# One-hot positions laid out contiguously, the last converted weights made early, and the fetch of the lower keys written a round later, in a kernel of attention, routed experts and a shared FFN

## The chip, the cores and the metric

The kernel runs on one core of one Trainium2 chip. A core has five engines that each work through an instruction list of their own in order: TensorE (matrix products and the loads of their stationary weights), VectorE, ScalarE, GpSimd and SyncE, which here only issues transfers. Sixteen DMA engines move data between the chip's memory and the core's SBUF. The metric is the device time of one execution in microseconds, lower is better.

## What is computed

```python
def reference(**kwargs):
    attn_out = _attn_ref(**attn_kwargs)            # B, H, S, D = 4, 8, 576, 64
    B, H, S, D = attn_out.shape
    x = np.ascontiguousarray(attn_out.transpose(0, 2, 1, 3)).reshape(B * S, H * D)
    x = _moe_ref(x=x, **moe_kwargs)
    return _moe2_ref(x=x, **moe2_kwargs)

def _moe_ref(x, w_gate, w1, w2):
    N, D = x.shape                                  # 2304, 512
    E = w_gate.shape[1]                             # 8
    cap = N // E                                    # 288
    flat = (x @ w_gate).flatten()
    order = np.argsort(-flat)
    ...                                             # greedy: best pair first, each token once, cap tokens an expert
    for e in range(E):
        mask = assigned == e
        h = np.maximum(x[mask] @ w1[e], 0.0)        # 512 x 1024
        out[mask] = h @ w2[e]

def _moe2_ref(x, w_in, w_out):
    h = x @ w_in                                    # 512 x 2048
    relu6 = np.clip(h + 3.0, 0.0, 6.0)
    g = h * relu6 / 6.0
    return g @ w_out
```

The attention is causal and has a second, linear part (`M_prev`, `z_prev`) mixed in by a gate. The weights of the experts and of the shared FFN arrive as 64-bit words, and those of the FFN are turned into 32-bit ones by the kernel.

## The kernel before

The attention takes the first 295 us or so; then the first round of the routing, and from about 335 us on eight rounds, one for each expert that is settled in turn. Round `s` has two kinds of steps: eight of kind 0 (one block of 128 of the expert's 1024 hidden columns each) on its 288 tokens, then `y_in`, which copies the expert's output out of PSUM into four tiles `y`, then sixteen of kind 1 (a block of the shared FFN each). Every step multiplies into `h`, makes `g` from `h` on ScalarE, VectorE and GpSimd (`t` and `pc` on ScalarE, lines 1210 and 1211, `g` on VectorE, line 1212), and multiplies `g` into four accumulators `acc`. Round 0 works with whole fp32 weights `raw`, straight from their transfers, and on the side splits those of the FFN into a high and a low part (`split_w`: `w` or `WB`, ScalarE line 1105, GpSimd line 1106), which the later rounds fetch again (`w<-hl`, line 1102) or keep (`WB`). Later rounds use such pairs throughout.

Of the FFN's 32 weight tiles, 28 are converted during the attention and lie in DRAM as `wb`. The last four (steps 14 and 15) are converted in round 0 itself: `cv.rest` loads one (line 975), four VectorE instructions make its bits (lines 981 to 984), ScalarE its sign (line 990, `wa`), GpSimd the product (line 991). The list `conv` holds these four, and each step of the loop takes one from it (line 1317). `load` puts them in the list when the step's place among the four `raw` places is its turn; their outputs are these `raw` tiles.

The routing of round `s + 1` is a generator, `Router.phase`, that is advanced a bit in each step of round `s`. Its parts here: the keys of each expert are made (from round 2 on in `by_dram`: matmul `rw`, ScalarE copy `ks` line 759, a transfer `kd` line 760, and two transfers that broadcast the upper and the lower halves to all partitions, `rHw` and `rLw`, line 763, all issued by SyncE); `search` then finds each expert's bound in four passes over `rHw` and four over `rLw`, each a `rcmp` of 128 x 2304 on VectorE (line 715) with a few small ones behind it; then positions, and `ids_units`. That has `u0`, which makes `ua` and the one-hot tile `oc` (row name `roc`, line 936, in two halves), and `u2`, which multiplies them in 20 matmuls of a 128 x 96 weight and a 6-column operand (recorded at the helper's line 702). Its result, by lines 945 to 949, is `ids`, the token numbers; the tokens are then gathered (`xg`) and transposed (`x_in`). Also there: the next `rX` (line 695), its transposes `rx`, and their copy `rXT` (line 747).

The order of each engine's instructions is made by a scheduler that works from the order of the code, its own estimates of time and the places that tiles wait for. Engines wait for each other through semaphores.

## Time and profile before

| | us |
|---|---|
| runs | 1116.09, 1106.57, 1122.56 |
| median | 1116.09 |
| profiled execution, its own time | 1115.67 |
| its span in the profile | 1113.9 |
| TensorE busy | 972.9 |
| VectorE busy | 637.6 |
| GpSimd busy | 625.4 |
| ScalarE busy | 587.8 |

A row of the timeline has the start, the duration, the engine, the line, the operation, output<-inputs and how many instructions of that kind follow each other; a bracket at its end is the time that the engine stood idle before it and what it waited for. "Granted clock" is TensorE's, as a share of 2.4 GHz; 0.5 is its lower level, 1.2 GHz.

### The profile page before, as it was taken

The numbers are of one execution on the slowest core, as the hardware profiler recorded it, in microseconds if no ns is written. First come the engines' busy times: TensorE is split into PE (matmuls) and PEld (weight loads), VectorE is DVE, ScalarE is ACT, GpSimd is POOL, SyncE is SP. The second block draws the span as 40 slices with busy tenths as digits, with TensorE's granted clock in tenths as the row PEclk, the third lists the DMA queues.
The fourth block names the chain that finished last, engine by engine and source line by source line (L and its number), as shares of the span: only waits on it lengthen the run. The fifth ranks groups of instructions, "written<-read, shape, count | busy, mean of one in ns | idle before, by whom it ended". The sixth has DMA issues, their size and how long they took to land.

```text
span 1113.9 us, 19553 instructions
## 1 busy us (share of the span) xinstructions
PE 972.9 (87%) x6556; PEld 876.5 (79%) x6556; DVE 637.6 (57%) x1587; ACT 587.8 (53%) x1471; POOL 625.4 (56%) x595
## 2 busy tenths in 40 slices
PE   3899888988419798789989999799999999999997
PEld 3677666766317586589989989799899999999996
DVE  8688996897682956971873684566385300200300
ACT  5777786876312343344554563465445356456453
POOL 7657656671410464663675685476557458558454
PEclk9899999999658899788999999999999999999998
DMA  6888877887223577447628726823942741751540
GB/s 156 228 251 226 254 226 221 255 234 198 72 77 102 166 244 207 153 128 231 175 73 257 202 76 220 199 76 127 259 138 74 235 170 58 256 184 58 190 153 22
DMA packets 125011, 190.23 MB, mean 171 GB/s; under 512 B 22128, under 2 KB 72688, under 8 KB 124912
## 3 DMA queue, kind: packets, MB, share of 16 engines
q1 hardware_dynamic: 121152, 179.54, 54.1%
q0 software_dynamic: 3072, 9.44, 2.9%
q8 instruction: 52, 0.85, 0.3%
q14 instruction: 47, 0.39, 0.1%
q10 hardware_dynamic: 688, 0.02, 0.0%
HBM read 144.60 MB, written 25.61 MB: 153 GB/s over the span
## 4 chain that ended last, share of the span: by engine, by line
PE 56%; DVE 15%; DMA 10%; POOL 7%; issue 5%; ACT 4%; SPq 2%; POOLq 0%; DVEq 0%; ACTq 0%
PE h L1221 7%; PE h L1222 6%; PE h L1224 6%; PE acc L1115 6%; PE acc L1116 6%; PE acc L1114 6%; PE h L1198 3%; DMA w<-hl 3%; PE acc L1251 3%; PE rp L702 3%; DVE rcmp L715 2%; PE av L328 2%; POOL gl L1244 2%; POOL t L1242 2%; PE sc L246 1%
## 5 line engine op out<-in xcount | busy, mean ns | idle before, releaser
L1106 POOL TENSOR_TENSOR w<-raw,w 128x512 fp32r<-128x512 f32 x128 | 168.1, 1325 | 108.4 <-ACT w L1105 107.8
L1242 POOL TENSOR_TENSOR t<-t,pc 128x288 f32<-128x288 f32 x112 | 92.0, 823 | 110.6 <-ACT t L1241 110.6
L1115 PE MATMUL acc<-gl,w 128*128 128x288 f32 x448 | 131.8, 304 | 9.0 <-POOL gl L1244 9.0
L1235 DVE TENSOR_TENSOR gl<-t,gh 128x288 fp32r<-128x288 f32 x56 | 37.6, 675 | 172.4 <-ACT gh L1234 169.3
L1116 PE MATMUL acc<-gh,w 128*128 128x288 f32 x448 | 130.0, 300 | 0.0
L1114 PE MATMUL acc<-gh,w 128*128 128x288 f32 x448 | 114.8, 310 | 1.7 <-DVE yo L1156 1.7
L1105 ACT ACTIVATE w<-raw 128x512 fp32r<-128x512 f32 x128 | 80.0, 632 | 57.9 <-PE acc L1116 26.7
L1239 ACT ACTIVATE t<-h,rthree 128x288 f32<-128x288 f32 x112 | 56.1, 501 | 99.2 <-PE h L1224 72.2
L1244 POOL TENSOR_TENSOR gl<-t,gh 128x288 fp32r<-128x288 f32 x112 | 91.1, 819 | 30.7 <-ACT gh L1243 30.7
L282 ACT ACTIVATE P<-P,mx 128x128 f32<-128x128 f32 (+2 forms) x144 | 83.7, 582 | 39.2 <-DVE mx L267 37.0
L1115 PEld LDWEIGHTS acc<-gl,w 128*128 128x128 f32 x448 | 86.6, 193 | 12.1 <-POOL gl L1244 11.8
L1116 PEld LDWEIGHTS acc<-gh,w 128*128 128x128 f32 x448 | 86.5, 193 | 0.0
L1114 PEld LDWEIGHTS acc<-gh,w 128*128 128x128 f32 x448 | 79.0, 196 | 3.4 <-DVE yo L1156 2.4
L1243 ACT ACTIVATE gh<-t 128x288 fp32r<-128x288 f32 x112 | 49.7, 444 | 58.3 <-POOL t L1242 58.0
L246 PE MATMUL sc<-kh,qs 128*128 128x128 f32 (+3 forms) x128 | 50.0, 401 | 28.5 <-DVE qs L218 12.8
L1221 PE MATMUL h<-yh,w 128*128 128x288 f32 x224 | 64.1, 305 | 11.4 <-DMA w<-hl 9.1
L991 POOL TENSOR_TENSOR wf<-wa,wf 128x512 f32<-128x512 f32 x28 | 37.7, 1347 | 62.0 <-DVE cm L380 14.6
L1221 PE MATMUL h<-xh,w 128*128 128x288 f32 x224 | 67.5, 320 | 3.5 <-ACT xh L1145 2.8
L267 DVE CUSTOM_DVE_ANT_0 P<-sc,mask 128x128 f32<-128x128 f32 (+3 forms) x128 | 59.4, 479 | 12.8 <-PE sc L247 8.8
L1222 PE MATMUL h<-xh,w 128*128 128x288 f32 x224 | 65.8, 313 | 0.0
L1115 PE MATMUL acc<-gl,WB 128*128 128x288 f32 x224 | 64.2, 297 | 0.0
L1116 PE MATMUL acc<-gh,WB 128*128 128x288 f32 x224 | 63.9, 295 | 0.0
(308 smaller groups left out, 2972.5 us busy)
## 6 DMA issues: line engine op xcount, KB each, us to landing
w<-hl SPq DMA_DIRECT2D x112, 512.0 KB
raw<-in_moe_w_dram SPq DMA_DIRECT2D x128, 256.0 KB
kh<-knh SPq DMA_DIRECT2D x60, 144.0 KB
raw<-in_moe_w_in_dram SPq DMA_DIRECT2D x16, 512.0 KB
raw<-in_moe_w_out_dram SPq DMA_DIRECT2D x16, 512.0 KB
hl<-w SPq DMA_DIRECT2D x16, 512.0 KB
wb<-wf SPq DMA_DIRECT2D x28, 256.0 KB
raw<-wb SPq DMA_DIRECT2D x28, 256.0 KB
```

The costliest lines, as they stand in the source:

```text
L246: nc.tensor.matmul(sc[:, :w], x, KH[n][:, h, :w], start=True, stop=False)
L282: nc.scalar.activation(x[:, :w], x[:, :w], AF.Exp, bias=mx, scale=-1.0, accum_out=col)
L1105: nc.scalar.activation(hi, src, AF.Copy)
L1106: nc.gpsimd.tensor_tensor(lo, src, hi.bitcast(F32), op=OP.subtract)
L1114: nc.tensor.matmul(p, ah, bh, start=first, stop=False)
L1115: nc.tensor.matmul(p, ah, bl, start=False, stop=False)
L1116: rt.behind = nc.tensor.matmul(p, al, bh, start=False, stop=last)
L1221: nc.tensor.matmul(p, wk[k][0], x[k][0], start=(k == 0), stop=False)
L1222: nc.tensor.matmul(p, wk[k][1], x[k][0], start=False, stop=False)
L1224: rt.behind = nc.tensor.matmul(p, wk[k][0], x[k][1], start=False, stop=(k == KC - 1))
L1242: nc.gpsimd.tensor_tensor(t, t, pc, op=OP.mult)
L1244: nc.gpsimd.tensor_tensor(gl, t, gh.bitcast(F32), op=OP.subtract)
```

## The change

Five edits. (1) `oc` is laid out with its 96 columns innermost instead of the 20 positions, so the weights of one matmul of `u2` lie side by side; line 936 then broadcasts `c` along the innermost dimension. (2) The four last tiles of the FFN have places of their own (two in the conversion's pool, two of the tag `ob`), `conv` is filled at the start of round 0, and is taken from in steps from the second on; `load` no longer gives them `raw` places. (3) `y_in` of round 0 copies all four `y` on ScalarE. (4) `by_dram` hands the fetch of `rLw` back to its caller, who issues it after one more step of the search. (5) In `phase`, that step is a `yield` of its own in each round.

```diff
@@ -652,9 +652,9 @@
     def late(self, ctx, ps):
         self.ps, self.tags = ps, ("r", 2)
         self.con = ctx.enter_context(self.tc.tile_pool(name="rcon2", bufs=1))
-        self.tile("oc", [128, 96, self.NT * self.B], BF)
-        oc96 = self.tile("oc96", [128, 96, self.NT * self.B], BF)
-        self.nc.gpsimd.iota(oc96, pattern=[[1, 96], [0, self.NT * self.B]], base=0, channel_multiplier=0,
+        self.tile("oc", [128, self.NT * self.B, 96], BF)
+        oc96 = self.tile("oc96", [128, self.NT * self.B, 96], BF)
+        self.nc.gpsimd.iota(oc96, pattern=[[0, self.NT * self.B], [1, 96]], base=0, channel_multiplier=0,
                             allow_small_or_imprecise_dtypes=True)
 
     def keys(self, b):
@@ -746,7 +746,8 @@
         else:
             nc.scalar.activation(XT, pt[:, :S], AF.Copy)
 
-    def by_dram(self):
+    def by_dram(self, wait=False):
+
 
         nc, ps, E, B, S = self.nc, self.ps, self.E, self.B, self.S
         n = 2 * E * B
@@ -758,10 +759,16 @@
             self.mm(p[:n, :S // 2], self.RB.rearrange("p d e b -> p (d e b)"), self.XT[:, c], start=True, stop=True)
             nc.scalar.activation(ks[:, c], p[:n, :S // 2], AF.Copy)
         nc.sync.dma_start(kd.rearrange("d e b s -> (d e b) s"), ks)
-        for d, W in ((0, self.Hw), (1, self.Lw)):
+
+        def back(d, W):
             src = kd[d].rearrange("e b s -> e (b s)")
             nc.sync.dma_start(W.rearrange("p b s -> p (b s)"), bass.AP(
                 tensor=src.tensor, offset=src.offset, ap=[[B * S, E], [0, 128 // E], [1, B * S]]))
+        back(0, self.Hw)
+        low = lambda: back(1, self.Lw)
+        if wait:
+            return low
+        low()
 
     def early(self, ps, *tags):
 
@@ -822,11 +829,14 @@
             elif s < DIRECT:
                 yield from self.direct()
             else:
-                self.by_dram()
+                low = self.by_dram(True)
                 yield BACK
             half = SHARE if s == 0 else 0
             Hs = self.search(self.Hw, cap - half, self.rowH, 2 * half)
             next(Hs)
+            yield next(Hs)
+            if s >= DIRECT:
+                low()
             for y in Hs:
                 yield y
             Bv = self.found
@@ -933,13 +943,13 @@
                                     self.uv[:, :, None, :].to_broadcast([128, NJ, 3, 2]), op=OP.mult)
             h = NJ // 2
             for j in (slice(0, h), slice(h, NJ)):
-                nc.vector.tensor_tensor(self.oc[:, :, j], self.oc96[:, :, j],
-                                        c[:, None, j].to_broadcast([128, 96, h]), op=OP.is_equal)
+                nc.vector.tensor_tensor(self.oc[:, j], self.oc96[:, j], c[:, j, None].to_broadcast([128, h, 96]),
+                                        op=OP.is_equal)
 
         def u2():
             p = self.ps.tile([128, 512], F32, name="rp", tag="r", bufs=2)
             for j in range(NJ):
-                self.mm(p[:96, :6], self.oc[:, :, j], st["ua"][:, j].rearrange("p a u -> p (a u)"),
+                self.mm(p[:96, :6], self.oc[:, j], st["ua"][:, j].rearrange("p a u -> p (a u)"),
                         start=(j == 0), stop=(j == NJ - 1))
             sv = self.sv
             nc.vector.tensor_copy(sv[:, :3], p[:96, :6].rearrange("p (a u) -> p a u", u=2))
@@ -997,7 +1007,7 @@
         if i < n:
             self.load(i)
         if 1 <= i <= n:
-            f = self.pool.tile([128, 4, 128], I32, name="wf", bufs=2)
+            f = self.pool.tile([128, 4, 128], I32, name="wf", tag="wf", bufs=2)
             self.bits(f, i - 1)
             self.sign(f.bitcast(F32), f, i - 1)
             j = i - 1
@@ -1070,13 +1080,12 @@
         s, kind, f = order[j]
         if s and kind:
             return
+        if kind and 2 * f >= cv.pre:
+            return
         raw = raws[j] = [wp.tile([128, 512], F32, name=f"raw{u}", tag=f"raw{u}", bufs=RAW) for u in range(2)]
         if kind:
             for u in range(2):
-                if f < cv.pre // 2:
-                    nc.sync.dma_start(raw[u], cv.wb[:, f, u * 512:(u + 1) * 512])
-                else:
-                    conv.append(lambda u=u: cv.rest(raw[u], 2 * f + u))
+                nc.sync.dma_start(raw[u], cv.wb[:, f, u * 512:(u + 1) * 512])
             return
         if f == 0:
             reg[s] = nc.sync.value_load(reg[s][0:1, 0:1], min_val=0, max_val=E - 1)
@@ -1087,6 +1096,13 @@
 
     W = {}
     conv = []
+
+    def last_rows():
+
+        for f in range(cv.pre // 2, FB):
+            raws[FA + f] = [cv.pool.tile([128, 512], F32, name="wf", tag="wf", bufs=2) if f % 2 == 0 else
+                            act.tile([128, 512], F32, name="ob", tag="ob", bufs=2) for u in range(2)]
+            conv.extend(lambda f=f, u=u: cv.rest(raws[FA + f][u], 2 * f + u) for u in range(2))
 
     def split_w(i, part):
         s, kind, f = order[i]
@@ -1181,10 +1197,7 @@
         for o, p in enumerate(acc):
             if s == 0:
                 y.append(whole("y", f"y{o}", 1))
-                if o % 2:
-                    nc.vector.tensor_copy(y[o], p[:, :cap])
-                else:
-                    nc.scalar.activation(y[o], p[:, :cap], AF.Copy)
+                nc.scalar.activation(y[o], p[:, :cap], AF.Copy)
                 continue
             hl = parts("y", f"y{o}", 1)
             nc.scalar.activation(hl[0], p[:, :cap], AF.Copy)
@@ -1292,6 +1305,7 @@
     cv.behind = rt.last
     for _ in x_in(0):
         pass
+    last_rows()
 
     def step():
         hold[0] -= RATE[s > 0]
@@ -1314,7 +1328,7 @@
             while pend:
                 second()
         ahead(i)
-        if conv:
+        if conv and i:
             conv.pop(0)()
         e = (l1 if s else l1_whole)(kind, f, X[s, 1] if kind else XT[s], W.pop((i, 0)) if s else raws[i][0],
                                     rt.behind if kind and f == 1 else None)
```

VectorE, at the search that runs in the second half of round 0; `raw0` and `raw1` are the outputs of the conversion, `rcmp` the passes, `g` a step's product. Before, from the fourth pass on:

```order
L715 TENSOR_SCALAR rcmp_178,cnt_4949<-rHw_176,T_4917 128x2304
L723 TENSOR_SCALAR rG_139<-T_4917,rcz_138 128x1
L1212 SCALAR_TENSOR_TENSOR g_4975<-t_4976,pc_4977 128x288
L981 TENSOR_SCALAR raw1_4911<-raw_4235 128x512
L724 STREAM_TRANSPOSE rrowH_146<-cnt_4949 128x32
L982 SCALAR_TENSOR_TENSOR raw1_4911<-raw_4235,raw1_4911 128x512
L983 TENSOR_SCALAR raw_4235<-raw_4235 128x512
L727 SCALAR_TENSOR_TENSOR fl_4953,T_4954<-rrowH_146,rG_139 128x33
L844 SCALAR_TENSOR_TENSOR m_5005<-rrowH_146 128x128
L984 TENSOR_SCALAR raw1_4911<-raw_4235 128x512
```

and with the change, at the same two passes:

```order
L715 TENSOR_SCALAR rcmp_178,cnt_4946<-rHw_176,T_4926 128x2304
L723 TENSOR_SCALAR rG_139<-T_4926,rcz_138 128x1
L724 STREAM_TRANSPOSE rrowH_146<-cnt_4946 128x32
L1225 SCALAR_TENSOR_TENSOR g_5050<-t_5051,pc_5052 128x288
L727 SCALAR_TENSOR_TENSOR fl_4950,T_4951<-rrowH_146,rG_139 128x33
L715 TENSOR_SCALAR rcmp_178,cnt_4972<-rHw_176,T_4951 128x2304
L723 TENSOR_SCALAR rG_139<-T_4951,rcz_138 128x1
L724 STREAM_TRANSPOSE rrowH_146<-cnt_4972 128x32
L727 SCALAR_TENSOR_TENSOR fl_4976,T_4977<-rrowH_146,rG_139 128x33
L854 SCALAR_TENSOR_TENSOR m_5019<-rrowH_146 128x128
L843 TENSOR_SCALAR rcmp_178<-rHw_176,T_4977 128x2304
```

The conversion (lines 981 to 984, now 991 to 994) no longer stands among the passes; `g` still stands behind a pass.

ScalarE, at the end of the expert's steps of round 0, where the four `y` are copied; `WB` and `w1` are weight splits. Before:

```order
L1105 ACTIVATE WB_4129<-raw0_4475 128x512
L1187 ACTIVATE y_4494<-acc0_4347 128x288
L1105 ACTIVATE WB_4129<-raw1_4430 128x512
L1187 ACTIVATE y_4498<-acc2_4349 128x288
L1105 ACTIVATE w1_4582<-raw1_4457 128x512
L1105 ACTIVATE WB_4129<-raw1_4476 128x512
```

and with the change:

```order
L1200 ACTIVATE y_4530<-acc0_4369 128x288
L1200 ACTIVATE y_4532<-acc1_4370 128x288
L1121 ACTIVATE WB_4129<-raw1_4466 128x512
L1200 ACTIVATE y_4534<-acc2_4371 128x288
L1121 ACTIVATE w1_4618<-raw1_4493 128x512
L1200 ACTIVATE y_4536<-acc3_4372 128x288
```

`y1` and `y3` joined the two others; one split stands between `y1` and `y2`, one between `y2` and `y3`.

At the head of round 0, on ScalarE, where `x` is the copy of the gathered tokens and `wa` the sign of a conversion. Before:

```order
L718 ACTIVATE rcmp_178,below_4038<-rLw_177,T_4034 128x864
L718 ACTIVATE rcmp_178,below_4048<-rLw_177,T_4044 128x864
L747 ACTIVATE rXT_179<-rx_4288 128x576
L1139 ACTIVATE x_4241<-xt_4237 128x288
L1139 ACTIVATE x_4253<-xt_4249 128x288
L1206 ACTIVATE g_4282<-h_4277 128x288
L1206 ACTIVATE g_4312<-h_4295 128x288
```

and with the change:

```order
L718 ACTIVATE rcmp_178,below_4038<-rLw_177,T_4034 128x864
L718 ACTIVATE rcmp_178,below_4048<-rLw_177,T_4044 128x864
L1155 ACTIVATE x_4241<-xt_4237 128x288
L1000 ACTIVATE wa_4344<-raw_4235 128x512
L1155 ACTIVATE x_4253<-xt_4249 128x288
L1000 ACTIVATE wa_4393<-raw_4306 128x512
L1000 ACTIVATE wa_4422<-raw_4347 128x512
L1121 ACTIVATE WB_4129<-ob_4263 128x512
L1219 ACTIVATE g_4286<-h_4281 128x288
```

Three signs and a split now stand ahead of the first `g`, and `rXT`, which stood ahead of it, does so no longer. The VectorE instructions of all four conversions went with them, to the places behind `ids` and `rX` of round 0. On SyncE the order did not follow the fourth edit: in rounds 2 to 5 the fetch of `rLw` is still the issue directly behind that of `rHw`, and in round 6 one transfer of split weights stands between the two.

## Rows read from the trace of the kernel before

**Rows 1.** The page: span; busy time, share and instructions of each engine.

```profile
span 1113.9 us, 19553 instructions
...
PE 972.9 (87%) x6556; PEld 876.5 (79%) x6556; DVE 637.6 (57%) x1587; ACT 587.8 (53%) x1471; POOL 625.4 (56%) x595
```

**Rows 2.** TensorE's waits: total us, times, longest us.

```profile
PE acc L1251 <- DVE g L1212: 8.3, 3, 3.9
```

**Rows 3.** Stretches: busy us (instructions) by engine, granted clock, DMA share, GB/s.

```profile
core 0: us, PE busy (x) PEld busy (x) DVE busy (x) ACT busy (x) POOL busy (x), PEclk, DMA share, GB/s
340.00:357.00 17.00, 17.00 (x70) 12.78 (x69) 0.00 (x0) 4.23 (x10) 0.00 (x0) 0.92 0.25 77
377.00:387.00 10.00, 6.62 (x13) 4.37 (x14) 9.82 (x23) 2.91 (x7) 3.71 (x3) 0.50 0.25 79
437.00:480.00 43.00, 30.02 (x109) 23.06 (x108) 36.42 (x70) 16.05 (x37) 22.74 (x19) 0.76 0.48 148
480.00:520.00 40.00, 36.67 (x235) 35.00 (x234) 24.49 (x51) 14.52 (x34) 18.20 (x16) 0.87 0.61 193
...
882.00:885.40 3.40, 3.40 (x17) 3.40 (x16) 0.00 (x0) 0.00 (x0) 2.44 (x3) 0.51 0.55 146
```

**Rows 4.** TensorE's weight loads at L702: duration min/median/max in ns.

```profile
L702 PEld LDWEIGHTS <-roc x160: 244/266/269, 327.5 to 880.6; 128*96 128x96 bf16 x160
...
L702 PEld LDWEIGHTS <-rUV x24: 94/97/291, 321.7 to 870.6; 128*128 128x128 bf16 x24
```

**Rows 5.** TensorE's timeline: start, duration in us, operation; then `u2` of round 3.

```profile
324.87 0.22 PE L702 MATMUL rp<-tot,rUV 128*128 128x1 bf16 x3 [2.77 <-DVE tot L888]
327.53 3.58 PE L702 MATMUL rp<-ua,roc 128*96 128x6 bf16 x20 [2.44 <-DVE roc L936]
...
589.73 0.60 PE L1165 MATMUL ot<-ident,yo 128*96 128x128 f32 x4
590.17 3.47 PE L702 MATMUL rp<-ua,roc 128*96 128x6 bf16 x20
```

**Rows 6.** VectorE's timeline around `u2` of rounds 0 and 3.

```profile
326.81 1.23 DVE L936 TENSOR_TENSOR roc<-roc,c 128x960 bf16<-128x960 bf16 x2 [0.15 <-DVE c L930]
...
334.32 0.82 DVE L695 TENSOR_TENSOR rX<-rB,roh 128x640 bf16<-128x640 bf16 x1
...
587.59 1.22 DVE L936 TENSOR_TENSOR roc<-roc,c 128x960 bf16<-128x960 bf16 x2
```

**Rows 7.** TensorE's timeline in round 0: two waits, in brackets.

```profile
379.65 2.29 PE L1198 MATMUL h<-y,raw 128*128 128x288 f32 x4 [4.87 <-DVE y L1185]
...
447.27 4.21 PE L1251 MATMUL acc<-g,raw 128*128 128x288 f32 x8 [3.90 <-DVE g L1212]
```

**Rows 8.** ScalarE's timeline in round 0, waits in brackets.

```profile
344.15 0.41 ACT L1206 ACTIVATE g<-h 128x288 f32<-128x288 f32 x1 [4.72 <-PE h L1198]
...
377.19 0.63 ACT L1105 ACTIVATE WB<-raw 128x512 fp32r<-128x512 f32 x1 [3.91 <-DMA raw<-wb]
...
441.52 0.63 ACT L1105 ACTIVATE w<-raw 128x512 fp32r<-128x512 f32 x1 [7.53 <-DMA raw<-wb]
```

**Rows 9.** VectorE, 437 to 480 us, by line and form: count, busy us, mean ns.

```profile
L715 DVE TENSOR_SCALAR_CACHE_REDUCE rcmp<-rHw,T 128x2304 uint16<-128x2304 uint16 x3 | 7.8, 2612 | 0.1
...
L982 DVE SCALAR_TENSOR_TENSOR raw<-raw,raw 128x512 int32<-128x512 int32 x3 | 2.0, 678 | 0.0
L984 DVE TENSOR_SCALAR raw<-raw 128x512 uint16<-128x512 int32 x3 | 1.9, 648 | 0.0
...
L983 DVE TENSOR_SCALAR raw<-raw 128x512 int32<-128x512 int32 x3 | 1.3, 420 | 0.0
L981 DVE TENSOR_SCALAR raw<-raw 128x512 int32<-128x512 int32 x3 | 1.2, 416 | 0.0
```

**Rows 10.** SyncE's issue of `rHw` and VectorE's first pass over it.

```profile
426.15 0.70 SPq L763 DMA_DIRECT2D rHw<-kd  x1
...
433.78 2.61 DVE L715 TENSOR_SCALAR_CACHE_REDUCE rcmp<-rHw,rT 128x2304 uint16<-128x2304 uint16 x1 [1.91 <-DMA rHw<-kd]
```

## The prediction

> **What bounds the kernel now.** I read the page first: TensorE is busy 87% of a span of 1113.9 us, no other engine over 57% [rows 1]. So a gain must come from TensorE's own time: shorter instructions, shorter idle stretches, or a higher granted clock. The list of TensorE's waits says where it idles in the expert stage: for VectorE's `g` in round 0, three times, 8.3 us in all [rows 2]. The busy times by stretch separate the stages [rows 3]. From 340 to 357 us TensorE is full while VectorE does nothing. From 437 to 480 it is busy 30.0 us of 43, at a mean clock of 0.76, while VectorE is at its busiest. From 377 to 387 the clock is at 0.50, that is 1.2 GHz. The same level stands in short stretches of 3.4 us: six such follow one operation, the gather of token numbers `u2`, between 414 and 885 us, and the last of them is in [rows 3]. Last I went to the durations of the instructions that the diff touches.
>
> **Contiguous one-hot positions.** `u2` is 20 pairs of weight load and matmul, in each of 8 rounds. Its 160 weight loads of 128x96 bf16 have a median of 266 ns, and a load of 128 columns that lie side by side has 97 [rows 4]. The first reads its columns 20 elements (40 bytes) apart. On the timeline one `u2` takes 3.47 to 3.58 us, 0.17 a pair, while the three `rUV` pairs took 0.22 us, 0.073 a pair, and the four fp32 transposes 0.44 us up to the next start, 0.11 a pair [rows 5]. With contiguous weights I take 0.085 a pair, nearer the bf16 row: 1.7 us a `u2`, a gain of 1.75. In round 0, whose start is on VectorE's `roc`, and in two more like it, the new layout costs something: the compare at L936 now has the broadcast operand innermost. Its two halves take 1.23 us in all; the product L695, which reads such an operand, takes 0.82 us for 640 elements, so 960 would take 1.2 us [rows 6], 0.55 more for each half. In those three rounds the first half is 0.55 late and the second lands 1.75 after the old start; ten pairs behind it end at 2.6 instead of 3.5, a gain of 0.9. In the other five VectorE was ahead: round 3's two halves took from 587.59 to 588.81, and its `u2` began at 590.17 [rows 5, 6]. There two halves of 1.2 would end at 589.99, still before `u2`, so the compare is hidden; without that cover a round gains 0.85 less. Sum: 5 x 1.75 + 3 x 0.9 = **-11.5 us**. Bounds: with 0.073 a pair -14; with 0.11 a pair -8; if the load does not shorten, 3 x 0.55 = +1.5.
>
> The row gives 266 ns at a distance of 40 bytes against 97 contiguous. [...]
>
> Against the change speaks the compare, which the rows price at 1.2 us. [...]
>
> **The clock behind `u2`.** Six of eight `u2` are followed by 3.4 us at 1.2 GHz [rows 3]. Such a stretch does half of what it would at 2.4, so it loses 1.7 us, 10.2 in all. [...] I take three to four of the six: **-6 us**, bounds 0 and -10.
>
> **The four `y` of round 0 on ScalarE.** TensorE waits 4.87 us at 374.8 for a `y` that VectorE copies [rows 7]; VectorE is full there (9.82 of 10 us, rows 3). After, all four copies are on ScalarE, but the second order above shows `y2` still behind the weight split `WB<-raw1`, which before waited 3.91 us for its DMA and began at 377.19 [rows 8]. If that DMA lands when it did, `y0` and `y1` are done before it and give TensorE some 1 us of work, to 375.8; `y2` comes at 378.2 (377.19 + 0.63 and a copy of 0.4). TensorE then waits 2.4 us instead of 4.87: -2.5. The clock of 0.50 from 377 to 387 may end earlier, where each microsecond gives back half: I add -1.5, **-4 us**; bounds -1 (the DMA later) and -8 (the split's DMA no longer late).
>
> **The last four converted tiles, out of the end of round 0.** Each has four VectorE instructions; the three tiles that fall in the stretch from 437 to 480 cost it 1.2 + 2.0 + 1.3 + 1.9 = 6.4 of 36.4 busy us [rows 9]. ScalarE loses the signs and waits less on loads: at 441.52 it had stood 7.53 us for `raw<-wb` with the next `t` and `pc` behind it [rows 8], and TensorE stood 3.90 us for the `g` made from those [rows 7]. The first order above shows the same `g` behind one search pass, not behind passes and conversions. The stretch idles 13.0 us of 43 on TensorE; the next, 480 to 520, idles 3.3 of 40 [rows 3], which in 43 would be 3.6, so 9.4 us of idle is particular to it. The search stays: eight passes of 2.61 us, 20.9 in all, in a row on VectorE, with the `g` of the last steps between them. I take a bit over half of the 9.4, and nothing for the clock: **-6 us**; bounds +6 (search and `g` collide as before and late weights come on top) and -12 (with the clock at 0.87 instead of 0.76, worth 30.0 x 0.11 / 0.87 = 3.8 more).
>
> **The same tiles at the head of round 0.** They land where VectorE was empty (0.00 of 17 us) and DMA at 0.25 of its time [rows 3]. What they delay is ScalarE: before, the first `g` ran at 344.15 [rows 8], with only copies ahead of it; now three signs and one split stand ahead of it (third order above), the last two tiles loading only when a place comes free. One load was waited for 3.91 us [rows 8]. With the h matmuls of the first two steps as cover I take 2 us of delay, half of such a wait: **+2 us**; bounds 0 and +6. Late behind it is `rXT`, with which round 1's keys begin; the first `g` and `rXT` share ScalarE's order.
>
> **The lower keys.** As the part on the change says, the fetch of `rLw` still stands directly behind that of `rHw`. SP issues `rHw` at 426.15, and the search waits 1.91 us for it until 433.78 [rows 10]. Moving nothing, it costs **0**; had the fetch been moved, those 1.9 us in five rounds, some 10 us, would bound the gain.
>
> **Sum.** -11.5 - 6 - 4 - 6 + 2 = -25.5, from the execution's own 1115.67 us: **1090 us**. The median of the three runs is 1116.09, 0.4 us above it; they spread from 1106.57 to 1122.56, so that about 2% (22 us, below 1093.8) is what a measurement of this kernel can tell from no change. The main case has its own range, 1080 to 1096.
>
> **Rivals.**
> 1. `u2` shortens, but the clock drops behind it as before, and the search's passes still decide when the last `g` of round 0 come: -11.5 for `u2`, -2 for the `y`, 0 for the rest, 1102 us. For it: the wait for `g` at 443.4 stands behind a pass in both orders. Against it: ScalarE's 7.53 us.
> 2. TensorE is the only bound: everything shrinks to its lower bound, -14 - 10 - 8 - 12 + 0 = -44, 1072 us. For it: 87% busy. Against it: `y2` and the search.
> 3. The change of layout does nothing to the load: 96 columns cost 266 ns for another reason. Then +1.5, 0 for the clock, -4 - 6 + 2, together -6.5: 1109 us. Against it: 97 ns for 128 columns.
> 4. The other side: the four tiles form one chain ahead of the first `g`, each a load (3.91 us by the wait in rows 8), VectorE's four operations (2.1) and a sign with its product, about 7 us a tile. In the worst case 28 us on TensorE's path at 340 instead of 2; 1090 + 26 = 1116, and with the gain behind `u2` not coming either 1122. It decides from 26 us of stall on. Against it: two tiles are loaded in the attention, and VectorE and DMA are free.
>
> **Chances.** Main case 0.50, of which 0.12 lies above 1093.8; rival 1 0.25; rival 2 0.15; rival 3 0.06; rival 4 0.04. Faster by over 2%: 0.38 + 0.15 = 0.53. Slower by over 2% (above 1138) needs rival 4 and more: 0.03. Within: 0.44. The range 1068 to 1107 holds most of the main case and of rivals 1 and 2; it leaves out rivals 3 and 4 and some 0.1 at the edges of the others, 0.2 in all.
>
> **What would show it.** Weight loads of `roc` near 80 to 100 ns and `u2` at 1.6 to 1.9 us, or the first step is wrong; granted clock near 1 behind `u2`; L936 at 2.4 us; the wait of TensorE at 374 to 380 down to about 2.4 us, with ScalarE waiting for `raw<-wb` ahead of `y2`; fewer than 8 us idle from 437 to 480; the first `g` at 346 to 347; `rLw` still issued within a microsecond of `rHw`. The sum is wrong above all if the clock behaves otherwise, or if 340 to 374 holds a new wait of more than 6 us.

## The result, and the profile after

The changed kernel takes 1099.63 us (median of 4 runs, 1097.07 to 1104.64), the kernel before 1117.36 in the same comparison: a ratio of 0.985 with a 95% interval of 0.981 to 0.990, that is 1.5% or some 16.5 us faster. Ratios, here and below, leave out executions more than 1.5% above the fastest of their kernel, and are not the quotients of the medians. The forecast was 1090 us, in a range of 1068 to 1107. The profiled execution is the slowest of the four, 1104.64 us.

The page of the changed kernel, its span and first row, and four rows of TensorE's waits between 320 and 1110 us (total, times, longest; the longest of all, 25.8 us for the search's last result, was 26.1 before):

```profile
span 1102.9 us, 19555 instructions
...
PE 950.7 (86%) x6556; PEld 852.3 (77%) x6556; DVE 652.8 (59%) x1585; ACT 589.0 (53%) x1473; POOL 630.9 (57%) x595
```

```profile
...
PE xt L1149 <- DMA xg<-x_dram,ids: 9.2, 2, 8.4
...
PE acc L1264 <- DVE g L1225: 7.8, 3, 3.5
...
PE rp L702 <- DVE roc L946: 5.1, 7, 2.1
PE acc L1264 <- DVE rrowL L724: 4.3, 1, 4.3
```

Against [rows 1] TensorE is busy 22.2 us less (972.9 to 950.7), but the span is only 11.0 us shorter: its idle time grew by 11.2, from 141.0 to 152.2 (span less busy time). Against [rows 2] the wait for `g` is nearly what it was (8.3 to 7.8), and a wait for `roc`, in seven places, has joined it.

The one-hot tile of the changed kernel: weight loads (min/median/max in ns), the compare, and two `u2` on TensorE's timeline:

```profile
L702 PEld LDWEIGHTS <-roc x160: 119/125/196, 331.2 to 871.8; 128*96 128x96 bf16 x160
...
L946 DVE TENSOR_TENSOR roc<-roc,c x16: 1146/1151/2440, 330.0 to 867.4; 128x960 bf16<-128x960 bf16 x16
```

```profile
331.25 2.03 PE L702 MATMUL rp<-ua,roc 128*96 128x6 bf16 x20 [2.94 <-DMA raw<-in_moe_w_dram]
```

```profile
593.75 1.02 PE L702 MATMUL rp<-ua,roc 128*96 128x6 bf16 x20 [1.12 <-DVE ob L1184]
```

The median load went from 266 ns [rows 4] to 125, the compare from 0.65 us a half to 1.15, and `u2` from 3.58 and 3.47 us [rows 5] to 2.03 in round 0, where it waits for the compare's second half, and 1.02 in round 3. The eight `u2` together: 28.0 us before, 12.3 after.

By stretch, in the columns of [rows 3] and moved along with the kernel: the head of round 0, the `y`, the end of round 0, the stretch behind it, and ten microseconds from the start of the last `u2`:

```profile
core 0: us, PE busy (x) PEld busy (x) DVE busy (x) ACT busy (x) POOL busy (x), PEclk, DMA share, GB/s
345.00:362.00 17.00, 15.69 (x58) 11.72 (x59) 7.17 (x13) 6.12 (x13) 6.60 (x5) 0.86 0.23 78
385.20:395.20 10.00, 6.35 (x22) 4.45 (x23) 9.93 (x17) 4.65 (x12) 5.19 (x4) 0.94 0.54 182
448.00:491.00 43.00, 28.47 (x134) 22.45 (x133) 37.83 (x70) 15.31 (x36) 20.35 (x17) 0.88 0.48 136
491.00:531.00 40.00, 37.08 (x270) 35.75 (x270) 20.13 (x43) 16.81 (x42) 19.40 (x20) 0.91 0.72 222
...
871.00:881.00 10.00, 9.63 (x86) 9.40 (x84) 2.50 (x8) 3.73 (x11) 2.80 (x3) 1.00 0.92 309
```

The head is no longer full (15.69 of 17 us busy, 17.00 before). The end of round 0 idles 14.5 us of 43, more than the 13.0 of before, at a better clock (0.88 instead of 0.76). Behind the last `u2` the clock stays at 1.00, where before it stood at 0.51 for 3.4 us.

### The profile page after: what moved, and what is told of

It reads as the page before. It is cut to its first block, busy times and chain, and to the rows that moved or that the text cites. A ratio compares the mean times of both kernels' runs of the same rounds, so it can differ in the third digit from the quotient of the medians.

```text
span 1102.9 us, 19555 instructions
## 1 busy us (share of the span) xinstructions
PE 950.7 (86%) x6556; PEld 852.3 (77%) x6556; DVE 652.8 (59%) x1585; ACT 589.0 (53%) x1473; POOL 630.9 (57%) x595
## 4 chain that ended last, share of the span: by engine, by line
PE 48%; DVE 19%; DMA 12%; POOL 8%; issue 7%; ACT 5%; SPq 1%; POOLq 0%; DVEq 0%; ACTq 0%
PE h L1234 6%; PE h L1235 6%; PE acc L1131 6%; PE h L1237 6%; PE acc L1132 5%; PE acc L1130 5%; DVE rcmp L715 3%; DMA w<-hl 3%; PE av L328 3%; PE acc L1264 2%; POOL w L1122 2%; POOL gl L1257 2%; PE h L1211 2%; POOL t L1255 2%; DVE P L267 1%
## 5 line engine op out<-in xcount | busy, mean ns | idle before, releaser
L1248 DVE TENSOR_TENSOR gl<-t,gh 128x288 fp32r<-128x288 f32 x56 | 41.6, 746 | 149.7 <-ACT gh L1247 148.4
L1132 PE MATMUL acc<-gh,w 128*128 128x288 f32 x448 | 128.8, 297 | 0.0
L1130 PE MATMUL acc<-gh,w 128*128 128x288 f32 x448 | 113.1, 305 | 1.7 <-DVE yo L1172 1.7
L1257 POOL TENSOR_TENSOR gl<-t,gh 128x288 fp32r<-128x288 f32 x112 | 91.2, 819 | 30.7 <-ACT gh L1256 30.7
L1132 PEld LDWEIGHTS acc<-gh,w 128*128 128x128 f32 x448 | 85.4, 191 | 0.0
L1130 PEld LDWEIGHTS acc<-gh,w 128*128 128x128 f32 x448 | 77.3, 192 | 3.3 <-DVE yo L1172 2.4
L1001 POOL TENSOR_TENSOR wf<-wa,wf 128x512 f32<-128x512 f32 x30 | 40.4, 1347 | 65.7 <-DVE cm L380 10.8
L1234 PE MATMUL h<-xh,w 128*128 128x288 f32 x224 | 64.8, 309 | 0.1
L715 DVE TENSOR_SCALAR_CACHE_REDUCE rcmp<-rHw,rT 128x2304 uint16<-128x2304 uint16 (+1 forms) x7 | 17.4, 2484 | 79.4 <-DMA rHw<-kd 59.3
L328 PE MATMUL av<-PT,vn 128*64 128x320 f32 (+4 forms) x462 | 64.0, 404 | 0.0
```

Of the source, the lines that this page charges most:

```text
L328: nc.tensor.matmul(st[a][h * 64:(h + 1) * 64, q0 - a:q1 - a], V[n][:w, i, h * D:(h + 1) * D], PT[n][:w, h, i, q0:q1] if i < NT - 1 else PT ...
L1130: nc.tensor.matmul(p, ah, bh, start=first, stop=False)
L1132: rt.behind = nc.tensor.matmul(p, al, bh, start=False, stop=last)
L1234: nc.tensor.matmul(p, wk[k][0], x[k][0], start=(k == 0), stop=False)
L1257: nc.gpsimd.tensor_tensor(gl, t, gh.bitcast(F32), op=OP.subtract)
```

## The experiments

Twelve kernels were run, each also timed against the kernel before. In the diffs, "before" or "changed" says which kernel the edit starts from. All ratios are to the kernel before, run beside each. e1 to e4, e5 to e8 and e9 to e12 were timed in three groups, each on a chip of its own, so kernels of different groups are compared by their ratios and not by their medians.

| run | starts from | what it is | median us | ratio, 95% interval |
|---|---|---|---|---|
| e1 | before | layout alone | 1101.84 | 0.990, 0.987 to 0.994 |
| e2 | before | early conversions alone | 1117.66 | 1.003, 1.000 to 1.007 |
| e3 | before | four `y` on ScalarE alone | 1113.20 | 0.998, 0.995 to 1.002 |
| e4 | before | fetch of the lower keys alone | 1116.08 | 1.002, 0.999 to 1.005 |
| e5 | changed | conversions behind step 9 | 1101.94 | 0.987, 0.983 to 0.992 |
| e6 | changed | conversions behind the token fetch | 1101.08 | 0.986, 0.982 to 0.990 |
| e7 | changed | positions in pairs | 1106.34 | 0.991, 0.988 to 0.994 |
| e8 | changed | conversions as before | 1098.30 | 0.985, 0.981 to 0.989 |
| e9 | e8 | pairs, cheaper constant tile | 1088.33 | 0.978, 0.973 to 0.984 |
| e10 | e8 | columns 20 bytes apart | 1116.25 | 1.002, 0.999 to 1.006 |
| e11 | e8 | `u2` done twice | 1110.72 | 0.997, 0.993 to 1.000 |
| e12 | changed | layout as before | 1119.01 | 1.001, 0.997 to 1.005 |

The next table is worked out from TensorE's timeline of one profiled execution of each. The stages are cut at starts of matmuls: the one that waits for the search's last result of round 0 (`rp<-rhs`, "attention" ends there), the first `h<-x`, the first and the last `h<-y` of round 0, and the first `h<-yh` of each later round. "Round k" is from one such start to the next, and "rest" ends with the start of the last matmul. The last two columns are the eight `u2` together, and the time from the first `h<-x` to 10 us ahead of the end that stands at a granted clock of 0.5. All in us. The traces give the clock as a share. What the prediction calls 1.2 GHz is a share of 0.50: in the kernel before, at 472 us, matmuls of 288 columns (`h<-xh,w`) start 0.24 us apart there, 1.2 columns a ns. Its 2.4 is a share of 1.00: at 344.92 us two matmuls of 512 columns (`rw<-rXT,rR`) start 0.21 us apart, some 2.4 columns a ns.

| kernel | attention | to first h | expert 0 | FFN 0 | to round 1 | round 1 | round 2 | round 3 | round 4 | rest | u2 | at clock 0.5 |
|---|---|---|---|---|---|---|---|---|---|---|---|---|
| before | 321.5 | 17.7 | 34.9 | 90.0 | 51.1 | 88.4 | 89.0 | 96.7 | 97.9 | 218.6 | 28.0 | 68.4 |
| e4 fetch | 326.9 | 17.9 | 35.0 | 90.3 | 51.4 | 89.9 | 88.5 | 93.1 | 99.7 | 218.4 | 28.0 | 68.5 |
| e2 early | 322.8 | 21.2 | 39.1 | 83.8 | 51.1 | 91.2 | 88.6 | 95.0 | 96.1 | 218.1 | 28.0 | 60.4 |
| e3 y | 322.9 | 17.7 | 35.0 | 86.9 | 50.1 | 91.2 | 88.6 | 98.5 | 97.9 | 218.1 | 27.8 | 65.2 |
| e12 no layout | 327.6 | 21.1 | 37.5 | 85.1 | 49.6 | 91.2 | 88.6 | 93.1 | 98.0 | 218.1 | 28.0 | 55.1 |
| e10 20 bytes | 325.9 | 17.6 | 35.7 | 85.2 | 46.6 | 88.4 | 88.8 | 96.5 | 99.6 | 218.0 | 27.3 | 56.3 |
| e1 layout | 324.0 | 17.3 | 35.1 | 97.1 | 47.2 | 89.4 | 88.2 | 88.2 | 90.0 | 218.3 | 11.3 | 55.1 |
| changed | 324.7 | 20.3 | 37.3 | 85.9 | 49.3 | 89.9 | 88.3 | 88.7 | 92.4 | 218.1 | 12.3 | 45.5 |
| e5 step 9 | 322.5 | 17.3 | 34.9 | 90.2 | 50.7 | 89.7 | 88.0 | 87.0 | 92.6 | 219.0 | 12.2 | 41.0 |
| e6 behind fetch | 322.0 | 19.9 | 36.7 | 82.4 | 49.9 | 89.7 | 86.4 | 92.4 | 90.3 | 219.4 | 12.0 | 38.7 |
| e7 pairs | 335.5 | 19.4 | 37.3 | 81.2 | 47.8 | 91.3 | 88.0 | 90.9 | 90.9 | 218.5 | 9.4 | 41.5 |
| e8 late | 322.7 | 17.4 | 34.6 | 86.3 | 47.8 | 89.9 | 87.2 | 87.8 | 92.6 | 219.4 | 11.3 | 40.4 |
| e9 pairs, cheap | 322.3 | 17.7 | 35.3 | 85.3 | 48.9 | 90.2 | 86.8 | 93.2 | 92.0 | 218.1 | 9.1 | 41.8 |
| e11 twice | 326.2 | 18.4 | 34.8 | 90.1 | 47.2 | 89.5 | 85.9 | 93.0 | 93.3 | 218.1 | 20.1 | 40.8 |

The table has one execution of each kernel. Stages that no edit is aimed at show how far two executions lie apart: attention from 322 to 328 (without e7, whose long iota lies there), round 3 from 93.1 to 98.5 among the kernels with columns 20 or 40 bytes apart. So a single difference of some 5 us shows nothing by itself; a smaller one is read only where it repeats in all kernels that share an edit. At the head it does: the five with the conversions there (changed, e2, e6, e7, e12) have 19.4 to 21.2 us to the first `h` and 36.7 to 39.1 in expert 0, the other nine 17.3 to 18.4 and 34.6 to 35.7.

### One edit at a time

e1, from before: the tile and its two uses.

```diff
-        self.tile("oc", [128, 96, self.NT * self.B], BF)
+        self.tile("oc", [128, self.NT * self.B, 96], BF)
...
-                nc.vector.tensor_tensor(self.oc[:, :, j], self.oc96[:, :, j],
-                                        c[:, None, j].to_broadcast([128, 96, h]), op=OP.is_equal)
+                nc.vector.tensor_tensor(self.oc[:, j], self.oc96[:, j], c[:, j, None].to_broadcast([128, h, 96]),
+                                        op=OP.is_equal)
```

> The kernel before with the contiguous one-hot tile alone. By the sum of the prediction: weight loads of roc near 100 to 125 ns, u2 at 0.8 to 1.8 us instead of 3.4, L936 at 1.15 us a half, -11.5 for u2 and -6 for the clock behind it, so about 17 us faster than before. By the rival, that the layout makes no difference by itself and the gain of the whole change comes from the moved conversions: within 5 us of before. If the trace after is read as 'layout alone makes nearly all of it', -15 us, and the half-clock stretches behind u2 are mostly gone.

By the ratio it is 11 us faster (0.990), less than the 17 expected and more than the rival's 5. `u2` fell to 11.3 us, rounds 3 and 4 to 88.2 and 90.0 us. But the FFN of round 0 took 97.1 us in the profiled execution, 7 more than before, with TensorE idle for 23.0 of them instead of 14.5. There VectorE began the search's first pass at 441.09, after 7.14 us without work, not 1.91 [rows 10], and the longest of TensorE's waits in that stage, 7.75 us, ends with a `g` that stands on VectorE behind a pass and a conversion (the row names the small instruction behind that `g`). VectorE's timeline in e1, three rows of it, and then TensorE's:

```profile
441.09 2.61 DVE L715 TENSOR_SCALAR_CACHE_REDUCE rcmp<-rHw,rT 128x2304 uint16<-128x2304 uint16 x1 [7.14 <-DMA rHw<-kd]
```

```profile
463.32 2.60 DVE L715 TENSOR_SCALAR_CACHE_REDUCE rcmp<-rLw,rT 128x2304 uint16<-128x2304 uint16 x1
...
466.05 0.44 DVE L984 TENSOR_SCALAR raw<-raw 128x512 uint16<-128x512 int32 x1
466.39 1.51 DVE L1212 SCALAR_TENSOR_TENSOR g<-t,pc 128x288 f32<-128x288 f32 x1
```

```profile
468.05 3.87 PE L1251 MATMUL acc<-g,raw 128*128 128x288 f32 x8 [7.75 <-DVE rrem L848]
```

So in this execution part of what the layout brings was lost where search and last steps met; whether every run of e1 loses it is not shown. Why the search came late here (its first pass 65 us behind the first `h<-y`, against 60 before) was not settled.

e2, from before: the places for the last tiles, filled at the head of round 0.

```diff
+    def last_rows():
+        for f in range(cv.pre // 2, FB):
+            raws[FA + f] = [cv.pool.tile([128, 512], F32, name="wf", tag="wf", bufs=2) if f % 2 == 0 else
+                            act.tile([128, 512], F32, name="ob", tag="ob", bufs=2) for u in range(2)]
+            conv.extend(lambda f=f, u=u: cv.rest(raws[FA + f][u], 2 * f + u) for u in range(2))
...
+        if kind and 2 * f >= cv.pre:
+            return
...
+    last_rows()
...
-        if conv:
+        if conv and i:
```

> The kernel before with the early conversions alone. By the sum of the prediction: -6 at the end of round 0 and +2 at its head, about -4 us. By the rival formed from the trace after: the first token fetch on GpSimd takes 3.9 us instead of 1.3 beside VectorE's conversions, the first x is 4 us late, round 1's routing runs 8 to 10 us later, and the end of round 0 gives that back but no more: 0 to +4 us.

The ratio is 1.003 (1.000 to 1.007): the rival's 0 to +4, not the sum's -4. By stage it is +3.5 to the first `h`, +4.2 in expert 0 and -6.2 in the FFN of round 0 (more on that stage below).

e3, from before:

```diff
-                if o % 2:
-                    nc.vector.tensor_copy(y[o], p[:, :cap])
-                else:
-                    nc.scalar.activation(y[o], p[:, :cap], AF.Copy)
+                nc.scalar.activation(y[o], p[:, :cap], AF.Copy)
```

> The kernel before with all four y copied on ScalarE, alone. By the sum of the prediction -4 us (the wait of 4.87 us at 375 down to about 2.4 us and some clock). By the rival, that the round's end is set by the search on VectorE, which these two copies only leave by 0.8 us: the wait goes and comes back at the g of the end of round 0, within 2 us of before.

0.998 (0.995 to 1.002). The FFN of round 0 is 3.1 us shorter, but the total can't be told from no change; between -4 and the rival's 2 us this run does not decide.

e4, from before: the second broadcast handed back to the caller.

```diff
-                self.by_dram()
+                low = self.by_dram(True)
                 yield BACK
...
             next(Hs)
+            yield next(Hs)
+            if s >= DIRECT:
+                low()
```

> The kernel before with the fetch of the lower keys written later, alone; the built order differs from before in one swap of two transfers on SyncE's queue in round 6. By the prediction 0 us, so within 3 us of before; this run also shows how far two executions of nearly the same instruction order lie apart, stage by stage. By the rival that the swap matters: a changed wait for w<-hl between 800 and 810 us, at most 3.7 us either way.

1.002 (0.999 to 1.005), no difference that can be measured. In this kernel a swap of two issues on SyncE in round 6 is all that the edit does.

e12, from the changed kernel: e1's edit taken back.

```diff
-        self.tile("oc", [128, self.NT * self.B, 96], BF)
+        self.tile("oc", [128, 96, self.NT * self.B], BF)
...
-                self.mm(p[:96, :6], self.oc[:, j], st["ua"][:, j].rearrange("p a u -> p (a u)"),
+                self.mm(p[:96, :6], self.oc[:, :, j], st["ua"][:, j].rearrange("p a u -> p (a u)"),
```

> The changed kernel with the one-hot positions 40 bytes apart as before: early conversions, y on ScalarE and the written place of the fetch remain. If the layout carries the gain (theory): ratio to before 0.998 to 1.004, u2 at 3.4 to 3.6 us, stretches at 1.2 GHz behind u2 in rounds 4 to 7 again. If the other edits bring something once they are together (rival): 0.992 or less.

1.001 (0.997 to 1.005): the other four edits together bring nothing that can be measured. Without the layout no gain is left; TensorE is busy 968.2 us on this kernel's page, 17.5 more than in the changed kernel. `u2` is back at 28.0 us; of the stretches at half clock (0.5) behind the `u2` of rounds 4 to 7, which were expected again, two of four are there. What e1 lacks of the changed kernel (0.990 against 0.985) lies within the intervals.

### The conversions

e5 and e6, from the changed kernel: only what the conversions are ordered behind.

```diff
-        if conv and i:
+        if conv and i >= 9:
+            cv.behind = rt.behind
             conv.pop(0)()
```

```diff
-    cv.behind = rt.last
+    cv.behind = rt.fetch
```

> The changed kernel with the four conversions ordered behind the matmuls of step 9 and later of round 0, still in places of their own. If the conversions at the head of the round cost by delaying the token fetch and ScalarE (theory): the first x comes 17.3 to 18 us after the search's last result instead of 20.3, the expert's part of round 0 takes 35 us instead of 37.3, the end of round 0 keeps its 86 us, so 4 to 5 us faster than the changed kernel, ratio to before 0.980. If VectorE is as full from 385 to 425 us as at the end of the round (rival): the g of these steps wait for conversions, the end of round 0 takes 90 us or more and the total is that of the changed kernel or worse, 0.985 to 0.99.

> The changed kernel with the conversions ordered behind the issue of the token fetch instead of behind the token numbers. By the theory that GpSimd's first fetch (3.9 us instead of 1.3) is slowed by VectorE's conversions running beside it: the three issues take 1.0 to 1.4 us each again, the wait for xg falls from 8.4 to about 5 us and the first x is 3 us earlier, 2 to 3 us faster than the changed kernel in all. By the rival that the tokens are late because the transfers of the conversions and of round 0's weights use the DMA engines: no change of the wait.

GpSimd's timeline has the three issues of the token fetch. In the changed kernel:

```profile
334.16 3.89 POOL L1073 DMA_INDIRECT xg<-x_dram,ids  x1 [22.44 <-DVE rleft L927]
338.36 0.95 POOL L1073 DMA_INDIRECT xg<-x_dram,ids  x1 [0.30 <-DVE rv L685]
339.61 0.92 POOL L1073 DMA_INDIRECT xg<-x_dram,ids  x1 [0.30 <-issue]
```

In e5:

```profile
331.92 1.34 POOL L1073 DMA_INDIRECT xg<-x_dram,ids  x1 [22.45 <-DVE rleft L927]
333.56 0.93 POOL L1073 DMA_INDIRECT xg<-x_dram,ids  x1 [0.30 <-issue]
```

In e6:

```profile
331.42 2.94 POOL L1073 DMA_INDIRECT xg<-x_dram,ids  x1 [22.45 <-DVE rleft L927]
334.67 1.04 POOL L1073 DMA_INDIRECT xg<-x_dram,ids  x1 [0.30 <-issue]
336.02 0.92 POOL L1073 DMA_INDIRECT xg<-x_dram,ids  x1 [0.30 <-DVE rv L686]
```

With the conversions right beside it the first issue takes 3.89 us, in e6 2.94, with none near 1.34, so the conversions do slow the fetch; e2, which has them there too, shows 3.89 again, before and e8, which don't, 1.34. By what way, the rows don't show. But e6 gained only 0.4 us to the first `h` (19.9 instead of 20.3): a miss of the 3 us expected. TensorE's first wait for tokens did fall, from 8.38 us to 5.96, but a second one grew from 0.85 to 2.84. Before, in the changed kernel and in e6:

```profile
335.54 0.90 PE L1133 MATMUL xt<-ident,xg 96*128 96x96 f32 x4 [4.44 <-DMA xg<-x_dram,ids]
336.64 0.91 PE L1133 MATMUL xt<-ident,xg 96*128 96x96 f32 x4 [0.20 <-DMA xg<-x_dram,ids]
```

```profile
341.65 0.90 PE L1149 MATMUL xt<-ident,xg 96*128 96x96 f32 x4 [8.38 <-DMA xg<-x_dram,ids]
343.41 1.54 PE L1149 MATMUL xt<-ident,xg 96*128 96x96 f32 x8 [0.85 <-DMA xg<-x_dram,ids]
```

```profile
336.49 0.90 PE L1149 MATMUL xt<-ident,xg 96*128 96x96 f32 x4 [5.96 <-DMA xg<-x_dram,ids]
340.23 1.54 PE L1149 MATMUL xt<-ident,xg 96*128 96x96 f32 x8 [2.84 <-DMA xg<-x_dram,ids]
```

So the issue on GpSimd is not all that holds the tokens up; the rival, transfers beside them, stays open for the rest. e5 gives the head back (17.3 and 34.9 us, as expected) and loses it in the FFN of round 0 (90.2 instead of 85.9), as its rival said: 0.987 (0.983 to 0.992), which holds the changed kernel's 0.985.

e8, from the changed kernel: `last_rows` and its two conditions taken back.

```diff
-        if kind and 2 * f >= cv.pre:
-            return
...
-                nc.sync.dma_start(raw[u], cv.wb[:, f, u * 512:(u + 1) * 512])
+                if f < cv.pre // 2:
+                    nc.sync.dma_start(raw[u], cv.wb[:, f, u * 512:(u + 1) * 512])
+                else:
+                    conv.append(lambda u=u: cv.rest(raw[u], 2 * f + u))
...
-    last_rows()
...
-        if conv and i:
+        if conv:
```

> The changed kernel with the conversions back at the end of round 0: layout, y and the written place of the fetch remain. If layout and conversions interact at the end of round 0 (theory from the layout alone, where that stage took 97 us instead of 90, and the changed kernel, 86): that stage takes 93 to 98 us and the total is that of the layout alone, ratio 0.990. If they only add up (rival): the stage takes about 88 us, and the ratio is that of the changed kernel less the 0.3% that the conversions alone cost, 0.982.

0.985 (0.981 to 0.989, which holds the rival's 0.982), and 86.3 us in the FFN of round 0: the rival was nearer, and the reading that early conversions are needed to cure the 97.1 us of e1 fell. With the other edits in, moving the conversions is worth nothing that can be measured.

### The layout, the load and the clock

e7, from the changed kernel: positions in groups of two, so a weight's columns lie 4 bytes apart and the compare reads two neighbouring positions innermost.

```diff
-        self.tile("oc", [128, self.NT * self.B, 96], BF)
+        self.tile("oc", [128, NQ, 96, 2], BF)
...
+                cq = c.rearrange("p (q a) -> p q a", a=2)
+                nc.vector.tensor_tensor(self.oc[:, j], self.oc96[:, j],
+                                        cq[:, j, None, :].to_broadcast([128, j.stop - j.start, 96, 2]),
+                                        op=OP.is_equal)
...
+                self.mm(p[:96, :6], self.oc[:, j // 2, :, j % 2], st["ua"][:, j].rearrange("p a u -> p (a u)"),
```

> The changed kernel with the one-hot positions in groups of two, so that the columns of a weight lie 4 bytes apart and the compare reads two neighbouring positions innermost. [...] If the compare is slow because its innermost operand has step 0: 0.65 us a half again instead of 1.15, and the waits for roc (5.1 us in 7) fall by 3 us or so: 0 to 3 us faster than the changed kernel.

The tile's rows in e7, load, compare and the constant tile:

```profile
L703 PEld LDWEIGHTS <-roc x160: 121/123/194, 341.5 to 877.3; 128*96 128x96 bf16 x160
...
L949 DVE TENSOR_TENSOR roc<-roc,c x16: 646/652/1950, 340.8 to 874.5; 128x960 bf16<-128x960 bf16 x16
L658 POOL IOTA roc<- x1: 10705/10705/10705, 311.8 to 311.8; 128x1920 bf16 x1
```

The load is as cheap as with neighbouring columns (123 ns for 125), and the compare, as expected, as cheap as before (0.65 us a half). The waits for `roc` came to 4.1 us in two places, 1 us less than in the changed kernel instead of 3. And the iota that fills the constant tile, with an innermost run of two, took 10.7 us on GpSimd, and the search of round 0 ended at 335.5 us. TensorE's wait there is 34.4 us, against 25.8 in the changed kernel, which is more than the total lost (0.991 against 0.985).

e9, from e8: e7's layout, and the constant tile by two iotas, each of runs of 96.

```diff
+        for r in range(2):
+            self.nc.gpsimd.iota(oc96[:, :, :, r], pattern=[[0, NQ], [1, 96]], base=0, channel_multiplier=0,
+                                allow_small_or_imprecise_dtypes=True)
```

> The kernel of the run with the conversions back at the end of round 0 (layout, all y on ScalarE), with positions in groups of two and the constant tile filled by two iotas of contiguous runs instead of the one that took 10.7 us. Theory: the search of round 0 ends at 322 to 325 us again instead of 335, the compare is 0.65 us a half, u2 takes 1.0 to 1.7 us without waiting for its second half, so 2 to 5 us faster than that kernel, ratio to before 0.980 to 0.983. Rival: the waits for the compare lie beside other waits in VectorE's list, and nothing is gained: 0.985.

```profile
L704 PEld LDWEIGHTS <-roc x160: 121/123/193, 328.3 to 866.7; 128*96 128x96 bf16 x160
...
L950 DVE TENSOR_TENSOR roc<-roc,c x16: 645/651/1940, 327.6 to 863.9; 128x960 bf16<-128x960 bf16 x16
L659 POOL IOTA roc<- x2: 1204/1534/1864, 308.1 to 309.2; 128x960 bf16 x2
```

Load, compare and iota are all cheap, `u2` is 9.1 us in all, and the time is the lowest measured: 1088.33 us, 0.978 (0.973 to 0.984). Against e8, from which it starts, and against the changed kernel that is 0.7% less by the ratios, whose intervals overlap a little, so a gain over them is likely and not shown. Where it would come from the profiles don't show: the profiled execution of e9 (1099.89 us) is its slowest and slower than that of e8 (1095.96), and waits for `roc` are 2.4 us in it against 2.1 in e8.

e10, from e8: groups of ten, 20 bytes.

```diff
-        self.tile("oc", [128, self.NT * self.B, 96], BF)
+        self.tile("oc", [128, NQ, 96, 10], BF)
```

> The same kernel with groups of ten, so that a weight's columns lie 20 bytes apart. [...] If the price grows with the distance (rival): between 125 and 266, near 190 ns, u2 near 2.4 us and a ratio near 0.99.

```profile
L703 PEld LDWEIGHTS <-roc x160: 240/261/263, 331.9 to 878.1; 128*96 128x96 bf16 x160
```

The load costs 261 ns at 20 bytes, as at 40, and 123 to 125 at 4 and 2. So the price does not grow with the distance as the rival had it (190 ns). Where between 4 and 20 bytes it rises was not run. The kernel is as slow as before, 1.002. Its own iota (6.2 us) has a part in that: TensorE waits 30.8 us for the search of round 0 there, 26.4 in e8. All four `u2` of rounds 4 to 7 are followed by a stretch at half clock again.

e11, from e8: the 20 matmuls twice.

```diff
-            for j in range(NJ):
+            for j in [*range(NJ)] * 2:
```

> The kernel with the conversions back at the end of round 0 and contiguous positions, with the 20 matmuls of u2 done twice over (the second time overwrites the first, the output stays the same). It holds VectorE's and the weight loads' prices and doubles the time with six-column matmuls. Theory, that the clock falls because of this time: the half-clock stretches behind u2 in rounds 4 to 7 come back, u2 takes 2.0 to 2.6 us, and the kernel is 8 to 15 us slower than the one with a single u2. If the clock is set by something else (rival): only the added 0.85 us a round, 7 us or less, and no stretches that were not there.

Some 13 us slower than e8 by the ratios (0.997 against 0.985), which lies in what the theory expected. But its mechanism is hardly there. In round 4 the 40 pairs take 2.2 us:

```profile
675.13 0.57 PE L702 MATMUL rp<-ua,roc 128*96 128x6 bf16 x10
675.87 1.51 PE L702 MATMUL rp<-ua,roc 128*96 128x6 bf16 x30 [0.16 <-DVE roc L946]
```

and no stretch at half clock follows; of the four `u2` in rounds 4 to 7 only that of round 6 is followed by one, and the kernel's sum at half clock is 40.8 us against e8's 40.4 in the profiled executions. Over all runs the mean granted clock is 0.938 against 0.942, so a small part of the clock may have been lost. `u2` itself is 8.8 us of the difference (20.1 against 11.3), near the rival's 7; the rest was not taken apart.

## Why the prediction was right, and where it was off

The range held the time, and the forecast of a gain held, but the point was 10 us too low, the main case's own range (1080 to 1096) missed, and of the three outcomes it came to the second: within 2%, held for 0.44, and not faster by more, held for 0.53. The sum came near by terms that missed to both sides.

**The one-hot positions** were the right first step, and too small: -11.5 forecast, -15.7 for `u2` in the trace (28.0 to 12.3). The load missed the 80 to 100 ns (125; no run shows one of 80, the shortest load of `roc` after the change is 119), but the pairs follow each other at 0.05 us (1.02 us for 20), less than one load takes, so neighbouring loads overlap; the 0.085 assumed from rows of other forms was too much. The compare came out as costed, 1.15 us a half for 1.2. Its cover was thinner than [rows 5, 6] suggested: waits for `roc` in seven places, 5.1 us, against 3.3 in two before, when `u2` itself was long enough to hide VectorE's second half.

**The clock** rose, and only in part where the step said. The prediction counted six stretches behind `u2` and took three to four of them away, an estimate with no run behind it. Four are gone, those of rounds 4 to 7; those of rounds 1 and 2 stayed, 6.8 us long each, and one behind round 3 is new. In us at half clock behind `u2` that is 17.1 instead of 23.9, worth 3.4 of the -6. For rounds 4 to 7 the count over all kernels is clear: with columns 20 or 40 bytes apart a stretch at half clock starts during `u2` or within 3 us of its end in 21 of 24 cases, with 2 or 4 bytes in 1 of 32.

The whole of it is more: in the six kernels with columns 20 or 40 bytes apart TensorE stands at half clock for 55 to 69 us, 62 in the mean; in the eight with 2 or 4 bytes for 39 to 55, 43 in the mean. The 19 us less, at half speed (eight `acc` of 288 columns take 4.21 us at a clock of 0.50 [rows 7] and 2.10 at 1.00, at 409.12 us), are worth some 10 us. 15 of them lie from round 1 on (27 us in the mean against 12); the time at half clock ahead of it varies with the other edits too. That the layout raises the clock is also seen over all runs: three pairs of kernels that differ in it have a mean granted clock of 0.931 and 0.940 (before, e1), 0.934 and 0.941 (e12, changed), 0.936 and 0.942 (e10, e8). Why is not shown. The theory of e11, that the time with six-column matmuls lowers the clock, is spoken against by that run, in which twice as many bring back one such stretch; but its `u2` are 1.9 to 2.7 us long in these rounds, shorter than the 3.4 to 3.6 of before. Whether it is the length of the loads or of `u2` as a whole stays open.

**The four `y`.** TensorE's wait fell from 4.87 us [rows 7] to 1.75, with `y2` behind a split that waited for its transfer, as the second order showed. Rows of ScalarE and of TensorE in the changed kernel:

```profile
384.27 0.63 ACT L1121 ACTIVATE WB<-raw 128x512 fp32r<-128x512 f32 x1 [2.46 <-DMA raw<-wb]
384.80 0.39 ACT L1200 ACTIVATE y<-acc 128x288 f32<-128x288 f32 x1
```

```profile
385.25 5.45 PE L1211 MATMUL h<-y,raw 128*128 128x288 f32 x20 [1.75 <-ACT y L1200]
```

The clock came back earlier too, as the step had it: in the 15 us behind the first `h<-y` a stretch of 6.8 to 10.2 us at half clock begins in the four kernels with two copies on VectorE (before, e1, e2, e4), and one of at most 3.4 in the ten with all on ScalarE. Alone the edit measures 0.998, with an interval that holds -4 us and 0.

**The conversions** are the step that failed, in sign: -4 forecast for both ends together, some +4 us measured alone (e2, 1.003). At the head +2 was forecast; the trace has +2.6 to the first `h`, in spite of a `u2` 1.55 us shorter, and +2.4 in expert 0, and alone (e2) +3.5 and +4.2, 7.7 in all and above the bound of +6. The prediction had costed ScalarE's order and the loads, and had said that VectorE and DMA are free there; it did not see that GpSimd's token fetch stands beside VectorE's conversions. TensorE's first transposes now waited 8.38 us for tokens, 4.44 before, a wait that no term of the sum had.

At the end of round 0 -6 was forecast, and e2 has -6.2 by stage; but that is luck. The term was for idle time, "and nothing for the clock". The FFN stage of round 0, before, in e2 and in the changed kernel, in the columns of [rows 3]:

```profile
374.13:464.16 90.03, 75.56 (x287) 56.62 (x286) 67.74 (x137) 33.64 (x71) 45.94 (x38) 0.87 0.63 192
```

```profile
383.13:466.98 83.85, 69.54 (x282) 52.66 (x280) 64.54 (x120) 31.03 (x68) 40.07 (x32) 0.92 0.62 193
```

```profile
382.28:468.17 85.89, 69.19 (x282) 51.00 (x280) 63.23 (x119) 31.58 (x69) 41.90 (x32) 0.92 0.62 193
```

TensorE is idle there for 14.5, 14.3 and 16.7 us: none of the idle time went. What fell is its busy time, by 6 us, at a granted clock of 0.92 instead of 0.87. And ScalarE's wait for `raw<-wb`, 7.53 us in [rows 8], did not go but became 10.89 in e2 and 9.67 in the changed kernel. ScalarE's row in e2, then ScalarE's and SyncE's rows in the changed kernel:

```profile
454.44 0.63 ACT L1111 ACTIVATE WB<-raw 128x512 fp32r<-128x512 f32 x1 [10.89 <-DMA raw<-wb]
```

```profile
454.75 0.63 ACT L1121 ACTIVATE WB<-raw 128x512 fp32r<-128x512 f32 x1 [9.67 <-DMA raw<-wb]
```

```profile
440.97 0.69 SPq L765 DMA_DIRECT2D rHw<-kd  x1
441.77 0.61 SPq L765 DMA_DIRECT2D rLw<-kd  x1
442.48 0.40 SPq L1088 DMA_DIRECT2D raw<-wb  x1
```

That weight is issued at 442.48, right behind the two broadcasts, and is used 12 us later. The prediction read the wait as the conversions' and not as that of the transfers ahead of it. That the broadcasts hold it up is argued from the order of the issues; a kernel in which `rLw` really goes later was not run.

**The lower keys**: 0 forecast, 1.002 measured.

**The rivals.** The first, 1102 us with the search still deciding the end of round 0, comes nearest by its time, but half by accident: the idle time at that end did stay (14.5 us of 43), while the clock, which it left as it was, rose, and the head took part of that back. On the pages TensorE is 22.2 us less busy. Behind the attention it is 27.0 less, about what the first two terms give at their true size; in the attention, where of the five edits only the iota lies, this execution happens to be busy 4.8 us more. The idle time that came back, 11.2 us, lies mostly in three stages: 5.1 us between the search's last result and the first `h`, where the tokens are waited for, 1.3 in expert 0, and 4.4 from the first `h<-y` to round 1.
